# Recurrence and experts on one core: the turn of the keys moved ahead by most of a step, and the last token lists cut in two

## Chip, cores and metric

The kernel runs on one core of a Trainium2 chip, as one launch. The metric is the device time in microseconds (us). Engines are named as in the profile: PE (TensorE matmul) and PEld (its weight loads), DVE (VectorE), ACT (ScalarE), POOL (GpSimd) and SP (SyncE, whose queue issues most DMAs).

## What is computed

Two stages in sequence. A recurrence over 768 positions for 4 batches and 8 heads of width 48, and a mixture of 8 experts over the 3072 tokens that it gives, with at most one expert for each token:

```python
for t in range(S):                                   # attention, per batch and head
    cur = np.einsum('bhd,bhe->bhde', u[None] * kt, vt)
    y[:, :, t] = np.einsum('bhd,bhde->bhe', rt, state + cur)
    state = w[None, :, :, None] * state + np.einsum('bhd,bhe->bhde', kt, vt)
x = y.transpose(0, 2, 1, 3).reshape(B * S, H * D)
do_compute = x @ w_skip > 0                          # the other tokens pass unchanged
e_idx = np.argmax(x @ w_gate, axis=1)                # expert; its gate is the softmax value
y = gate_w[:, None] * (np.maximum(x @ w1[e], 0.0) @ w2[e])
out = x + y                                          # for the computed tokens
```

## The kernel before

**Steps.** The recurrence is cut into 12 chunks of 64 positions and two groups of heads, so 24 steps (`m` from 0 to 23). In a step PE makes `scores` (keys against queries, L503, into `ps_p`), `across` (queries against the carried state `sblk`, L563, into `ps_y`), `within` (masked scores `am` against the values `vkv`, L547, into `ps_y`) and `state` (keys against values, L527, into `ps_s`). POOL scales keys (`prep_t`: `kt`, L458) and queries (`prep_r`: `rd`, L443); ACT adds the scaled second half of `rd` (`prep_u`, L455), copies the finished rows (`take_x`: `xt`, L583) and the state (`sblk`, L540). PE turns the scaled keys into the bank `ps_t` (`turn_k`, L470) and DVE copies them to `kd` (`take_k`, L474), from which the scores two steps on are made; the first two keys are turned unscaled (`turn_raw`, L480) and scaled in the copy. DVE copies the scores under two masks (`mask_scores`, L514 and L515). Decay tables `w_d` are grown on DVE (L351) and turned by PE (`turn_table`, L362).

**Beside the steps.** The x of a finished chunk is written to the output by SP (L596), and also turned by PE (`turn_x`, L609, into `ps_t`) and copied by ACT (`xT`, L612). For every four tiles of 128 tokens come the logits (L623), copied, turned back and copied again (L631, L635, L636). A generator `route` (`tick` advances it: "v" pieces on DVE, "p" pieces on PE) then makes a token list of them: choice, ranks through matmuls into `pr`, one-hot rows `ol` and `vl`, and a matmul into `mine`, added to `lists`; `place` writes ids for the gathers (`gid`, `sid`) and the gates. `ROUTES` says at which step which tiles are listed. Expert 0's weights are loaded in 12 pieces during the steps and split into a high and a low part (ACT `whi`, POOL `wlo`, L123 and L124), expert 1's are loaded in steps 20 to 23.

**Bridge.** Behind step 23 the first 128 tokens of expert 0 are computed by the generator `first` (`single`: W1 at L210, turns L222, W2 L232, DVE's `hl` L225, `mix` L185), between the pieces of the last two lists; the second 128 tokens (`second`) need the last gather (L142). Expert 1 is split meanwhile (L134, L135, two pieces of three on DVE) and its tokens turned (`turn_one`, L162 to L164). The order of work is the order of the code: each engine takes its instructions in program order. The eight PSUM banks of the steps serve the experts too.

**Experts 1 to 7.** W1 at L171, rectifier at L175 and L176, W2 at L181, mix, and scatters (L188); the next expert is split beside it.

## Time and profile before

| | us |
|---|---|
| three runs | 310.77, 312.38, 317.28 (median 312.38) |
| the profiled execution | 311.63 |
| its span, first to last instruction | 309.8 |
| PE, DVE, ACT, POOL busy in the span | 273.6, 178.2, 138.4, 150.1 |

The profiled execution is 1.83 us longer than its span. Rows of the trace give the start in us from the span's start, the length, the engine, the line, the operation, output and inputs, and in brackets how long the engine idled before it and what ended that. PEclk is the clock that TensorE was granted, as a share of full speed.

### The profile page before, as it was taken

Reading aid. Unit: us, or ns where it says so; the run is one execution under the profiler, and the core shown is the slowest. Engines: PE = TensorE matmul, PEld = TensorE weight load, DVE = VectorE, ACT = ScalarE, POOL = GpSimd, SP = SyncE. Lnnn points to the kernel's source line nnn. Section 1 sums busy time; section 2 is a strip of 40 time slices with the busy share of each in tenths; the row PEclk is TensorE's granted clock in tenths of the full one; section 3 lists DMA queues with packets and bytes.
Section 4 is the critical chain, followed back from the end, with each engine's and each line's share of the span. In section 5 each row is a group of like instructions: output and inputs, shape, how many; then the busy total and the mean of one; then the engine's idle time right before and its main releaser. Section 6 shows DMA issues by size and latency. Waiting matters only on the chain.

```text
span 309.8 us, 9701 instructions
## 1 busy us (share of the span) xinstructions
PE 273.6 (88%) x4065; PEld 242.3 (78%) x4066; DVE 178.2 (58%) x377; ACT 138.4 (45%) x318; POOL 150.1 (48%) x159
## 2 busy tenths in 40 slices
PE   8699999899876997597976889999999999999991
PEld 3487767677765876475664779999999999999991
DVE  4536445445756376755573869486764938376310
ACT  4235545465533364323333738172654728173200
POOL 8366774748465264504136866435353444534111
PEclk9979999999997599959997999999999999999997
DMA  7368678788785263627993459571908355000000
GB/s 212 94 184 236 185 215 237 208 251 241 227 238 131 76 172 123 175 54 247 278 367 88 122 151 329 182 304 40 406 19 294 129 203 245 25 16 24 15 23 27
DMA packets 24582, 52.64 MB, mean 170 GB/s; under 512 B 3732, under 2 KB 11951, under 8 KB 24528
## 3 DMA queue, kind: packets, MB, share of 16 engines
...
q14 instruction: 19, 0.16, 0.2%
q10 hardware_dynamic: 272, 0.05, 0.1%
...
## 4 chain that ended last, share of the span: by engine, by line
PE 69%; DVE 15%; ACT 5%; issue 4%; DMA 4%; SPq 1%; POOL 0%; POOLq 0%; DVEq 0%
PE ps_p L503 10%; PE ps_s L171 10%; PE ps_y L181 9%; PE ps_p L181 9%; PE ps_p L171 5%; PE ps_y L171 5%; DVE kd L474 4%; PE ps_s L527 3%; PE ps_t L609 3%; PE ps_y L547 2%; PE ps_y L271 2%; DMA raw<-in_w_dram 2%; DMA xg<-out_dram,gid 2%; PE ps_t L470 2%; ACT rd L455 2%
## 5 line engine op out<-in xcount | busy, mean ns | idle before, releaser
L135 POOL TENSOR_TENSOR wlo<-raw,whi 128x512 fp32r<-128x512 f32 x28 | 37.8, 1348 | 39.2 <-ACT whi L134 20.2
L135 DVE TENSOR_TENSOR wlo<-raw,whi 128x512 fp32r<-128x512 f32 x56 | 50.5, 922 | 5.1 <-ACT whi L134 5.1
L134 ACT CAST whi<-raw 128x512 fp32r<-128x512 f32 x84 | 47.4, 624 | 0.0
L503 PE MATMUL ps_p<-rd,kd 48*64 48x128 f32 x768 | 30.6, 295 | 14.6 <-DVE kd L474 13.9
L514 DVE COPY_PREDICATED am<-below,ps_p 128x512 f32<-128x512 int8 x24 | 17.7, 738 | 36.7 <-PE ps_p L503 36.7
L503 PEld LDWEIGHTS ps_p<-rd,kd 48*64 48x64 f32 x768 | 24.0, 144 | 18.4 <-issue 11.7
L188 POOL DMA_INDIRECT out_dram<-xg,sid x16 | 17.4, 1087 | 35.5 <-DVE xg L185 30.1
L124 POOL TENSOR_TENSOR wlo<-raw,whi 128x512 fp32r<-128x512 f32 x12 | 15.6, 1299 | 38.2 <-ACT whi L123 35.4
L612 ACT COPY xT<-ps_t 128x384 f32<-128x384 f32 x23 | 11.0, 480 | 45.8 <-PE ps_t L609 45.8
L458 POOL TENSOR_TENSOR kt<-dm,w_t 128x384 f32<-128x384 f32 x24 | 24.4, 1019 | 13.5 <-ACT w_t L365 6.6
L142 POOL DMA_INDIRECT xg<-out_dram,gid x16 | 17.6, 1098 | 26.7 <-DVE em L788 12.2
L443 POOL TENSOR_TENSOR rd<-dm,w_d 112x512 f32<-112x512 f32 x22 | 29.0, 1318 | 0.0
L171 PE MATMUL ps_s<-xh,whi 128*128 128x256 f32 x84 | 23.8, 283 | 0.0
L171 PE MATMUL ps_s<-xl,whi 128*128 128x256 f32 x84 | 23.8, 283 | 0.0
L171 PE MATMUL ps_s<-xh,wlo 128*128 128x256 f32 x84 | 23.8, 283 | 0.0
L455 ACT ACTIVATE rd<-rd,uw 112x256 f32<-112x256 f32 x48 | 21.7, 505 | 2.3 <-POOL rd L443 2.3
L175 ACT ACTIVATE hh<-ps_p 128x512 fp32r<-128x512 f32 x7 | 4.2, 598 | 40.7 <-PE ps_p L171 40.7
L474 DVE COPY kd<-ps_t 112x512 f32<-112x512 f32 x22 | 15.1, 686 | 11.3 <-PE ps_t L470 5.6
L527 PE MATMUL ps_s<-vkv,kt 128*48 128x96 f32 x352 | 20.4, 262 | 0.0
L181 PE MATMUL ps_p<-whi,hh 128*128 128x384 f32 x56 | 19.3, 345 | 0.0
L181 PE MATMUL ps_y<-whi,hl 128*128 128x384 f32 x56 | 18.8, 336 | 0.0
L181 PE MATMUL ps_p<-wlo,hh 128*128 128x384 f32 x56 | 18.8, 336 | 0.0
...
## 6 DMA issues: line engine op xcount, KB each, us to landing
...
xg<-out_dram,gid POOLq DMA_INDIRECT x16, 3.5
out_dram<-xg,sid POOLq DMA_INDIRECT x16, 2.8
...
```

The source lines that it names most:

```text
L134: nc.scalar.copy(hi[:, s], t[:, s])
L135: (eng or nc.vector).tensor_tensor(lo[:, s], t[:, s], hi[:, s].bitcast(F32), ALU.subtract)
L142: ins = nc.gpsimd.indirect_dma_start(out=xg, out_offset=None, in_=out, in_offset=bass.IndirectOffsetOnAxis(ap=gid[:, q : q + 1], axis=0), ...
L171: nc.tensor.matmul(ph, a[:, c, fs], b[:, c, :], start=(k == 0), stop=(k == 3 * NCC - 1))
L181: nc.tensor.matmul(py, a, b[:, f, :], start=(k == 0), stop=(k == 3 * NFC - 1))
L443: eng.tensor_tensor(rd[:, :, :, 0], loaded[m][:DR, :RC].rearrange("p (n h c) -> p n h c", n=4, h=2), w_d[:, (m // NG) % NSUB, 0, half(m)][ ...
L455: nc.scalar.activation(rd[:, :, h, 1], rd[:, :, h, 0], AF.Copy, scale=uw[:, hp : hp + 1])
L458: nc.gpsimd.tensor_tensor(kts[m % 4][:, :, :, :D], loaded[m][:, RC:].rearrange("p (q k d) -> p q k d", q=NPAIR, d=D), w_t[:, (m // NG) % N ...
L474: nc.vector.tensor_copy(kds[m].rearrange("p k n c -> p (k n c)"), ps_t[:DR, :])
L503: nc.tensor.matmul(ps_p[lo(n), b, 2 * k * C : 2 * (k + 1) * C], kd[lo(a, D), k, n], rd[lo(a, D), NPAIR * b + q, h].rearrange("p s c -> p ( ...
L514: nc.vector.copy_predicated(shape(am[m % 2]), below, p[:, :, 0])
L527: nc.tensor.matmul(ps_s[g][lo(a, D), k * W2 : (k + 1) * W2], kt[:, q, 2 * h + a, :D], blocks[:, :, a, k], start=m < NG and k == 0, stop=Tr ...
```

## The change

The parts, in the order of the program:

- Warm-up matmuls on `ones`: 18 in a row become 9, and three before them two. In the opening the scores of step 0 come ahead of the table's turn; POOL builds the masks before it clears `kt`.
- The keys of the first four steps (`NRAW`), not two, are turned raw; their scaling copy is one instruction instead of two, with another order of heads in `kd`.
- A step is written in another order: across, turn of x, second half of `rd`, scores, masks, then at once turn and copy of k for step m+2, POOL's keys and queries, list matmuls, logits, within, `xt`, state, and the list work on DVE last.
- Lists are made of four tiles each, at steps 6, 10, 14, 18 and 22; before, the first was of eight, at step 11. `VTICKS` sets how many pieces a step takes.
- The last list (tiles 20 to 23) has a generator of its own: its logits are made with tokens on the partitions (`logits_here`), so they are not turned back, and its ids are placed and the two gathers issued before the gates are computed.
- The load of expert 2 waits for the second of these gathers.
- `first` runs to its end before `second` begins; behind it the PSUM pool is closed and eight new banks are declared for the experts.

```diff
-ROUTES = {11: (0, 8), 15: (8, 12), 19: (12, 16), 23: (16, 20)}
+ROUTES = {6: (0, 4), 10: (4, 8), 14: (8, 12), 18: (12, 16), 22: (16, 20)}
...
-NWARM = 18
+NWARM = 9
+NRAW = 4
+WARM1 = 4
+VTICKS = (2, 1, 3, 3)
...
         for j in range(pieces) if piece is None else (piece,):
-            (eng or nc.sync).dma_start(out=raw[e][:, j * q : (j + 1) * q], in_=w12[e, :, j * q : (j + 1) * q])
+            ins = (eng or nc.sync).dma_start(out=raw[e][:, j * q : (j + 1) * q], in_=w12[e, :, j * q : (j + 1) * q])
+            if after is not None:
+                tc.add_manual_dep(
...
-        for bank0 in (ps_t, ps_y[:, 0], ps_l):
+        for bank0 in (ps_t, ps_y[:, 0]):
             warm(1, bank0)
         warm(NWARM, ps_y[:, 1])
...
-        for t in kts:
-            nc.gpsimd.memset(t, 0.0)
-        clear_v(3, nc.gpsimd)
...
         below = lower("below", ALU.is_gt)
         eye = lower("eye", ALU.is_equal)
+        for t in kts:
+            nc.gpsimd.memset(t, 0.0)
+        clear_v(3, nc.gpsimd)
...
-            src = bank[:DR, :].rearrange("p (q h n c) -> p q h n c", q=2, h=2, n=2)
-            for h in range(2):
-                hp = (m % NG) * 2 + h
-                nc.vector.tensor_tensor(
...
+            nc.vector.tensor_tensor(
+                kds[m].rearrange("p (h q) n c -> p h (q n) c", h=2),
+                bank[:DR, :].rearrange("p (h q c) -> p h q c", h=2, c=C),
+                w_d[:, (m // NG) % NSUB, 1, half(m)].unsqueeze(2).to_broadcast([DR, 2, 4, C]),
+                ALU.mult,
+            )
...
-                        kd[lo(a, D), k, n],
+                        kd[lo(a, D), 2 * h + q if m < NRAW else k, n],
...
+        def logits_here(*ns):
+            for n in ns:
+                for c in range(NCC):
+                    nc.tensor.matmul(
+                        logit[:, (n % 4) * GW : (n % 4) * GW + E + 1],
+                        turned_x[n][:, c * P : (c + 1) * P],
...
-                if g1 == NT:
-                    place(1)
...
+        def last_route(g0, g1):
...
+            mx = small("mx")
+            nc.vector.tensor_reduce(mx, l8, AX.X, ALU.max)
+            nc.vector.tensor_tensor(eq[:, :, :E], l8, bc(mx), ALU.is_equal)
+            rdo = small("rdo", w=E)
...
+            yield
+            nc.tensor.matmul(pr[:, : n * E], tri, oh.rearrange(col), start=True, stop=False, skip_group_check=True)
...
+            vl = small("vl", F32R, NV3 * E)
+            ids = id1[:, g0:g1].unsqueeze(2).to_broadcast([P, n, E])
+            nc.vector.tensor_tensor(vl[:, :, :E], oh, ids, ALU.mult)
...
+            rk = small("rkp", w=E)
+            nc.vector.tensor_tensor(rk, pr[:, : n * E].rearrange("p (n e) -> p n e", e=E), oh, ALU.mult)
...
+            nc.vector.tensor_reduce(r1, rk, AX.X, ALU.add)
...
+            nc.vector.tensor_tensor(
+                ol, lane1[:, None, :].to_broadcast([P, n, P]), r1.unsqueeze(2).to_broadcast([P, n, P]), ALU.is_equal
+            )
...
+            for j in range(n):
+                nc.tensor.matmul(mine[:, :E], ol[:, j, :], vl[:, j, :E], start=(j == 0), stop=(j == n - 1))
...
+            last = lists[:, :, NJ - 1, :]
+            nc.vector.tensor_tensor(last[:, 0], mine[:, :E], last[:, 0], ALU.add)
+            place_ids(1)
+            yield
+            df = small("df", w=E)
+            nc.vector.tensor_tensor(df, l8, bc(mx), ALU.subtract)
+            nc.scalar.activation(df, df, AF.Exp)
+            nc.vector.tensor_scalar(over[:, g0:g1], r1, float(CAP), None, ALU.is_ge)
...
+            gw = small("gw")
+            nc.vector.tensor_reduce(gw, df, AX.X, ALU.add)
...
+            for v, val in ((1, gh), (2, gl)):
...
+            for j in range(n):
+                nc.tensor.matmul(
+                    mine[:, E : NV3 * E], ol[:, j, :], vl[:, j, E:], start=(j == 0), stop=(j == n - 1)
...
+            yield
+            nc.vector.tensor_tensor(
+                last[:, 1:], mine[:, E : NV3 * E].rearrange("p (v e) -> p v e", e=E), last[:, 1:], ALU.add
+            )
+            place_gates(1)
...
+        banks = {"py": [ps_p[:, 0]]}
...
         setup = setup_routes()
         turn_raw(0, ps_t)
         turn_raw(1, ps_y[:, 0])
-        turn_table(0, ps_l)
         prep_r(0, nc.vector)
         prep_u(0)
         take_raw(0, ps_t)
-        warm(4, ps_y[:, 1])
-        scores(0)
-        prep_t(0)
         prep_r(1, nc.vector)
         prep_u(1)
         take_raw(1, ps_y[:, 0])
+        scores(0)
+        turn_table(0, ps_l)
+        mask_scores(0)
+        grow(1)
+        warm(WARM1, ps_y[:, 1])
+        prep_t(0)
         prep_t(1)
         load_rk(3)
         load_v(2)
-        mask_scores(0)
-        grow(1)
-        turn_table(1, ps_l)
+        prep_r(2, nc.gpsimd)
         load_rk(4)
-        prep_t(2)
-        prep_r(2, nc.gpsimd)
         for m in range(NSTEP):
-            q = (m - 6) // 4
             if m + 3 < NSTEP:
                 load_v(m + 3)
             if m + 5 < NSTEP:
                 load_rk(m + 5)
+            across(m)
+            if m >= 2:
+                turn_x(m - 2)
+            if m + 2 < NSTEP:
+                prep_u(m + 2)
+            if m + 1 < NSTEP:
+                scores(m + 1)
+                mask_scores(m + 1)
+            if m + 2 < NRAW:
+                turn_raw(m + 2, ps_t)
+                take_raw(m + 2, ps_t)
+            elif m + 2 < NSTEP:
+                turn_k(m + 2)
+                take_k(m + 2)
+            if m < 3:
+                turn_table(1 + m, ps_l)
+                if m < 2:
+                    grow(2 + m)
+            if m == 0:
+                prep_t(2)
             if m + 3 < NSTEP:
                 prep_t(m + 3)
                 prep_r(m + 3, nc.gpsimd)
-            across(m)
-            if m + 1 < NSTEP:
-                scores(m + 1)
-                mask_scores(m + 1)
-            if m >= 2:
-                turn_x(m - 2)
+            tick("p")
+            if m >= 5 and m % 4 == 1:
+                logits((m - 5) // 4)
             if m >= 6 and m % 4 == 2:
-                logits(q)
-            if m >= 7 and m % 4 == 3:
-                logits_back(q)
-            tick("p")
-            if m + 2 < NSTEP:
-                prep_u(m + 2)
+                logits_back((m - 6) // 4)
             within(m)
             take_x(m)
             if m < NSTEP - NG:
                 state(m)
-            if m + 2 < NSTEP:
-                turn_k(m + 2)
-            if m in (0, 2):
-                grow(2 + m // 2)
-                turn_table(2 + m // 2, ps_l)
             if m in ROUTES:
                 begin_route(*ROUTES[m])
-            if m < 18:
-                tick("v", 2)
-            else:
-                tick("v", 3)
-                tick("p")
-                tick("v", 1)
-            if m + 2 < NSTEP:
-                take_k(m + 2)
+            tick("v", VTICKS[m % 4] + (m == NSTEP - 2))
...
+        last = last_route(NT - 4, NT)
+        next(last)
         run(1)
         turn_x(NT - 2)
         turn_x(NT - 1, ps_p[:, 1], nc.vector)
+        tick("p")
+        logits_here(20, 21)
+        tick("v", 4)
+        logits_here(22, 23)
+        take_logits(5, nc.vector)
+        assert not routes
+        next(last)
+        run(2)
+        next(last)
+        next(last)
         run(1)
-        tick("v", 4)
-        logits(5)
-        tick("p")
+        next(last)
+        next(last)
+        for q in (E, E + 1):
+            landed = gather(q, wpool)
         run(1)
-        tick("v", 4)
-        logits_back(5)
-        begin_route(NT - 4, NT)
+        next(last)
+        next(last)
         run(1)
-        tick("p")
...
+    def expert_banks():
+        pctx.close()
+        epsum = ctx.enter_context(tc.tile_pool(name="epsum", bufs=1, space=PSUM, reuse_waits="tile"))
+        for kind, k in (("ph", 4), ("pt", 2), ("py", 2)):
+            banks[kind] = [epsum.tile([P, 512], F32, name=f"{kind}{j}") for j in range(k)]
+            used[kind] = 0
 
...
-        load_expert(2, pieces=12)
+        load_expert(2, pieces=12, after=landed)
...
+            if g is second and n2 == 0:
+                for _ in first:
+                    pass
+                expert_banks()
...
-        for _ in first:
-            pass
```

How PE's order changes, in a plain step (before: step 4, after: step 8). In before, PE's queue has the turn of k (L470) behind state (L527):

```order
L563 MATMUL ps_y<-sblk_209,rd_370 64x48 x16
L503 MATMUL ps_p<-rd_438,kd_614 64x128 x16
L609 MATMUL ps_t<-ident,xt_498 128x128 x3
L547 MATMUL ps_y<-vkv_108,am_158 64x48 x16
L527 MATMUL ps_s_68<-vkv_108,kt_112 48x96 x8
L470 MATMUL ps_t<-ident,kt_114 112x128 x4
L563 MATMUL ps_y<-sblk_210,rd_438 64x48 x16
L503 MATMUL ps_p<-rd_538,kd_701 64x128 x16
```

In after, the same queue has it behind the scores (L477 behind L507; L567 is across, L612 the turn of x, L551 within, L531 state):

```order
L567 MATMUL ps_y<-sblk_199,rd_759 64x48 x16
L612 MATMUL ps_t<-ident,xt_880 128x128 x3
L507 MATMUL ps_p<-rd_860,kd_959 64x128 x16
L477 MATMUL ps_t<-ident,kt_114 112x128 x4
L551 MATMUL ps_y<-vkv_108,am_148 64x48 x16
L531 MATMUL ps_s_68<-vkv_108,kt_112 48x96 x8
L567 MATMUL ps_y<-sblk_200,rd_860 64x48 x16
L612 MATMUL ps_t<-ident,xt_880 128x128 x3
L507 MATMUL ps_p<-rd_962,kd_1071 64x128 x16
```

The turn of k moved from the end of the step to its middle, and the turn of x from behind the scores to ahead of them; both write `ps_t`.

DVE in a step with list work. In before, the copy `kd` (L474) is the last instruction of its step, behind the decay of the state (L537) and the list's comparisons:

```order
L514 COPY_PREDICATED am_159<-below,ps_p 128x512
L515 COPY_PREDICATED am_159<-eye,ps_p 128x512
L537 TENSOR_TENSOR ps_s_68<-ps_s_68,pw 112x384
L744 TENSOR_SCALAR hi_1648<-r_1545 128x8
L746 SCALAR_TENSOR_TENSOR lw_1650<-hi_1648,r_1545 128x8
L747 SCALAR_TENSOR_TENSOR hi_1648<-hi_1648,m_1437 128x8
L749 TENSOR_TENSOR ol_1647<-lane,lw_1650 128x1024
L474 COPY kd_1654<-ps_t 112x512
L514 COPY_PREDICATED am_158<-below,ps_p 128x512
L515 COPY_PREDICATED am_158<-eye,ps_p 128x512
```

In after, `kd` (L481) follows the two masks (L518, L519), and the list's operations (L764 to L774) stand behind it:

```order
L518 COPY_PREDICATED am_149<-below,ps_p 128x512
L519 COPY_PREDICATED am_149<-eye,ps_p 128x512
L481 COPY kd_1071<-ps_t 112x512
L764 TENSOR_TENSOR ol_1013<-lane,lw_1016 128x512
L769 TENSOR_TENSOR oj_1104<-blk,hi_1014 128x64
L774 TENSOR_TENSOR vl_1106<-oj_1104,id_195 128x4x16
L774 TENSOR_TENSOR vl_1106<-oj_1104,gh_1004 128x4x16
L774 TENSOR_TENSOR vl_1106<-oj_1104,gl_1005 128x4x16
L518 COPY_PREDICATED am_148<-below,ps_p 128x512
L519 COPY_PREDICATED am_148<-eye,ps_p 128x512
L481 COPY kd_1164<-ps_t 112x512
```

The copy passed the list work, which now stands ahead of the next masks instead.

DVE at the last list. In before, gates (`gl` L706, `gate_s` L790) and ids are made together:

```order
L708 TENSOR_TENSOR rkp_2674<-ps_l,oh_2647 128x32
L710 TENSOR_REDUCE r_2676<-rkp_2674 128x4
L723 TENSOR_TENSOR ol_2679<-lane_203,r_2676 128x512
L728 TENSOR_TENSOR vl_2681<-oh_2647,id_205 128x4x8
L728 TENSOR_TENSOR vl_2681<-oh_2647,gh_2670 128x4x8
L728 TENSOR_TENSOR vl_2681<-oh_2647,gl_2671 128x4x8
L738 TENSOR_TENSOR lists<-ps_l,lists 128x3x8
L786 TENSOR_SCALAR gid<-lists 128x8
L788 TENSOR_SCALAR em_2702<-lists 128x8
L789 SCALAR_TENSOR_TENSOR sid<-lists,em_2702 128x8
L790 TENSOR_TENSOR gate_s<-lists 128x8
L714 TENSOR_REDUCE sums_2678<-oh_2647 128x8
```

In after, the ids are summed (L863) and placed (L907 to L910) first, and the gates' operations (from L867) come behind:

```order
L851 TENSOR_TENSOR rkp_2687<-ps_l,oh_2672 128x32
L853 TENSOR_REDUCE r_2689<-rkp_2687 128x4
L855 TENSOR_TENSOR ol_2691<-lane_193,r_2689 128x512
L863 TENSOR_TENSOR lists<-ps_l,lists 128x8
L907 TENSOR_SCALAR gid<-lists 128x8
L909 TENSOR_SCALAR em_2704<-lists 128x8
L910 SCALAR_TENSOR_TENSOR sid<-lists,em_2704 128x8
L867 TENSOR_TENSOR df_2718<-lg,mx_2664 128x32
L869 TENSOR_SCALAR over<-r_2689 128x4
L872 TENSOR_REDUCE gw_2722<-df_2718 128x4
L873 TENSOR_SCALAR gw_2722<-gw_2722 128x4
L874 RECIPROCAL gw_2722<-gw_2722 128x4
```

What moved are the exponential, the gates' operations and two of the three products `vl`, from ahead of the ids to behind them.

## Rows read from the trace of the kernel before

**Rows 1.** The page's first line and its line on PE: busy us (share of the span), number of instructions.

```profile
span 309.8 us, 9701 instructions
PE 273.6 (88%) x4065; PEld 242.3 (78%) x4066; DVE 178.2 (58%) x377; ACT 138.4 (45%) x318; POOL 150.1 (48%) x159
```

**Rows 2.** The table of stages: stretch (us from the span's start), its length, then busy us (number of instructions) of PE, PEld, DVE, ACT and POOL, granted clock, mean busy share of the DMA engines, GB/s.

```profile
26.16:92.00 65.84, 59.58 (x1662) 47.90 (x1666) 35.71 (x66) 34.66 (x93) 41.18 (x44) 1.00 0.80 227
...
31.26:139.14 107.88, 92.82 (x2393) 75.38 (x2385) 62.09 (x138) 50.76 (x138) 57.87 (x54) 0.92 0.64 181
40.07:44.58 4.51, 4.18 (x119) 3.38 (x120) 2.18 (x3) 2.71 (x7) 3.48 (x4) 1.00 0.68 224
...
98.67:107.57 8.90, 8.90 (x131) 7.79 (x135) 3.06 (x10) 2.87 (x7) 0.83 (x1) 0.50 0.31 96
...
131.86:139.14 7.28, 7.07 (x120) 5.63 (x120) 4.20 (x14) 2.21 (x6) 0.00 (x0) 0.55 0.21 50
139.14:146.29 7.15, 5.58 (x164) 4.47 (x164) 3.29 (x16) 2.52 (x9) 2.34 (x3) 1.00 0.81 259
146.29:165.99 19.70, 13.90 (x106) 11.07 (x106) 11.08 (x52) 5.73 (x16) 6.35 (x6) 0.99 0.90 288
165.99:180.28 14.29, 11.93 (x57) 9.85 (x57) 11.12 (x13) 8.26 (x18) 11.76 (x10) 0.89 0.30 86
180.28:303.39 123.11, 123.07 (x877) 122.59 (x877) 73.80 (x115) 58.58 (x113) 51.30 (x41) 1.00 0.41 150
```

**Rows 3.** The chain that ended last, in two plain steps: start, us, what it was.

```profile
35.56 1.10 PE ps_p L503 x32
36.66 0.49 PE ps_t L609 x3
...
37.17 0.48 ACT xT L612
37.65 0.80 ACT rd L455 x2
38.46 0.37 ACT xt L583
...
39.23 0.70 DVE kd L474
...
40.07 1.10 PE ps_p L503 x32
```

**Rows 4.** Waits in the nineteen steps (31.26 to 139.14): who waited for whom, us in total, times, longest.

```profile
PE ps_p L503 <- DVE kd L474: 13.9, 18, 2.8
...
PEld ps_y L563 <- ACT xt L583: 1.2, 7, 0.2
```

**Rows 5.** The timeline of steps 17 to 22, PE's scores and DVE.

```profile
98.67 1.99 PE L503 MATMUL ps_p<-rd,kd 48*64 48x128 f32 x32 [2.83 <-DVE kd L474]
...
114.67 0.17 DVE L700 TENSOR_REDUCE gw<-df 128x4 f32<-128x32 f32 x1
...
116.68 1.00 DVE L747 SCALAR_TENSOR_TENSOR hi<-hi,m 128x4 f32<-128x4 f32 x1
...
118.21 0.68 DVE L474 COPY kd<-ps_t 112x512 f32<-112x512 f32 x1
...
119.03 1.10 PE L503 MATMUL ps_p<-rd,kd 48*64 48x128 f32 x32 [1.32 <-DVE kd L474]
...
120.19 0.73 DVE L514 COPY_PREDICATED am<-below,ps_p 128x512 f32<-128x512 int8 x1 [1.31 <-PE ps_p L503]
...
131.86 1.98 PE L503 MATMUL ps_p<-rd,kd 48*64 48x128 f32 x32 [1.60 <-DVE kd L474]
```

**Rows 6.** The timeline of the opening: PE and POOL.

```profile
2.77 5.32 PE L271 MATMUL ps_y<-ones 128*128 128x512 bf16 x18
...
8.02 1.08 PE L480 MATMUL ps_t<-ident,dm 128*48 128x128 f32 x16
...
15.36 1.60 PE L362 MATMUL ps_l<-ident,w_d 112*64 112x112 f32 x16 [2.35 <-DVE w_d L351]
...
17.55 1.00 POOL L458 TENSOR_TENSOR kt<-dm,w_t 128x384 f32<-128x384 f32 x1 [4.18 <-ACT w_t L365]
...
18.51 1.27 POOL L443 TENSOR_TENSOR rd<-dm,w_d 112x512 f32<-112x512 f32 x1
```

**Rows 7.** The last list in the timeline, from the last `xt` to the turned rows, and the page's line on the gathers (median us from issue to landing).

```profile
145.81 0.48 ACT L583 COPY xt<-ps_y 128x384 f32<-128x384 f32 x1 [0.18 <-PE ps_y L547]
...
158.70 0.17 DVE L786 TENSOR_SCALAR gid<-lists 128x8 uint32<-128x8 f32 x1
...
159.14 0.99 POOL L142 DMA_INDIRECT xg<-out_dram,gid  x1 [10.63 <-DMA raw<-in_w_dram]
...
164.87 0.55 PE L162 MATMUL ps_t<-ident,xg 128*128 128x128 f32 x3 [2.80 <-DMA xg<-out_dram,gid]
...
xg<-out_dram,gid POOLq DMA_INDIRECT x16, 3.5
```

**Rows 8.** The end of the bridge in the timeline: DVE and POOL.

```profile
176.73 2.40 DVE L135 TENSOR_TENSOR wlo<-raw,whi 128x512 fp32r<-128x512 f32 x1
177.28 1.30 POOL L135 TENSOR_TENSOR wlo<-raw,whi 128x512 fp32r<-128x512 f32 x1
...
180.06 0.60 DVE L185 SCALAR_TENSOR_TENSOR xg<-ps_y,gate_s,xg 128x384 f32<-128x384 f32 x1
```

More of the change, by code (lines that the diff above doesn't have):

```diff
@@ L73, in tile_wkv_moe @@
     wpool = ctx.enter_context(tc.tile_pool(name="wpool", bufs=1))
-    psum = ctx.enter_context(tc.tile_pool(name="psum", bufs=1, space=PSUM))
+    pctx = ExitStack()
+    psum = pctx.enter_context(tc.tile_pool(name="psum", bufs=1, space=PSUM))
     ps_p = psum.tile([P, 2, 512], F32, name="ps_p")
@@ L101, in tile_wkv_moe, with load_expert @@
     WCOLS = 2 * NCC * F
-    def load_expert(e, piece=None, pieces=4, eng=None):
+    def load_expert(e, piece=None, pieces=4, eng=None, after=None):
         if piece in (None, 0):
@@ L480, in turn_raw @@
                     nc.tensor.matmul(
-                        bank[lo(a, D), k * P : (k + 1) * P], src[:, k, a], ident, start=True, stop=True
+                        bank[lo(a, D), k * P : (k + 1) * P], src[:, k % 2, k // 2, a], ident, start=True, stop=True
                     )
@@ L542, in within @@
         def within(m):
-            t = vals_in[m]
+            t = vals_in.pop(m)
             for k in range(4):
@@ L615, in turn_x @@
             turned_x[n] = xT
-        LG = 64
-        back = ps_l[:, 384:]
+        logit, back = ps_l[:, 64:192], ps_l[:, 384:]
         def logits(q):
@@ L630, in logits @@
             lt = wk.tile([P, P], F32, tag="lt", name=f"lt{q}")
-            nc.scalar.copy(lt, ps_l[:, LG : LG + P])
+            nc.scalar.copy(lt, logit)
             turned_x["lt"] = lt
@@ L638, in logits_back, with take_logits @@
             )
-            seen[0] = 4 * q + 3
+        def logits_here(*ns):
[4 more added lines that the diff above has]
+                        turned_x[n][:, c * P : (c + 1) * P],
+                        wg_sb[:, c, : E + 1],
+                        start=c == 0,
+                        stop=c == NCC - 1,
+                    )
+        def take_logits(q, eng):
+            eng.tensor_copy(
+                lg[:, 4 * q : 4 * q + 4, :], logit.rearrange("p (j e) -> p j e", j=4)[:, :, : E + 1]
+            )
         NV3 = 3
@@ L784, in place, with place_gates, place_ids @@
+        def place(j):
+            place_ids(j)
+            place_gates(j)
+        def place_gates(j):
+            c = slice(j * E, (j + 1) * E)
+            nc.vector.tensor_tensor(gate_s[:, c], lists[:, 1, j], lists[:, 2, j], ALU.add)
+        def place_ids(j):
             c = slice(j * E, (j + 1) * E)
@@ L805, in tick @@
                     routes[0][1] = nxt
-        banks = {
-            "ph": [ps_s[0], ps_s[1], ps_p[:, 1], ps_y[:, 1]],
-            "pt": [ps_t, ps_l],
-            "py": [ps_p[:, 0], ps_y[:, 0]],
-        }
+        banks = {"py": [ps_p[:, 0]]}
         used = dict.fromkeys(banks, 0)
@@ L927, in tile_wkv_moe @@
         turn_x(NT - 1, ps_p[:, 1], nc.vector)
+        tick("p")
[8 more added lines that the diff above has]
+        next(last)
         run(1)
-        tick("v", 4)
-        logits(5)
-        tick("p")
+        next(last)
+        next(last)
+        for q in (E, E + 1):
+            landed = gather(q, wpool)
         run(1)
-        tick("v", 4)
-        logits_back(5)
-        begin_route(NT - 4, NT)
+        next(last)
+        next(last)
         run(1)
-        tick("p")
-        tick("v", 4)
-        run(2)
-        tick("p")
-        tick("v", 4)
-        run(2)
-        tick("p")
-        tick("v", 4)
-        run(1)
-        tick("p")
-        tick("v", 4)
-        assert not routes
-        gather(E, wpool)
-        gather(E + 1, wpool)
-        order = [q for e in range(2, E) for q in ((E + e,) if e < NEARLY else (e, E + e))]
+        next(last)
+        next(last, None)
+        order = [q for e in range(2, E) for q in ((E + e,) if e < NEARLY else (e, E + e))]
+    def expert_banks():
[4 more added lines that the diff above has]
+            used[kind] = 0
     with ExitStack() as mctx:
```

74 lines of the change are left out of this document (64 added, 10 removed).

## The prediction

> **What bounds the kernel now.** I read the page's first lines, then a table of stages, then the chain of waits inside two plain steps, then the waits that end late and the instructions around them. The span is 309.8 us, PE (TensorE) busy for 88% [rows 1]. The table cuts the span by what runs [rows 2]: an opening of 31.26 us, nineteen steps of the recurrence (from the scores of step 4 to those of step 23) of 107.88, a last step of 7.15, a bridge of 19.70 and 14.29 in which expert 0 is computed and the last rows are gathered, and the experts from 180.28 on. There PE is busy 123.07 of 123.11 us, and the change moves nothing in that stage or behind it. A gain has to come from before 180.28.
>
> In the nineteen steps PE is busy 92.82 of 107.88 us [rows 2]. Of the 15.06 that are idle one wait has 13.9: scores waiting for `kd`, the copy of the turned keys [rows 4]. The chain of a plain step shows why [rows 3]: scores, the turn of x, its copy `xT` on ACT (ScalarE), the scalings of `rd`, the copy `xt`, and only then, behind another ACT copy, DVE's (VectorE's) copy `kd` of 0.70 and the scores again, 4.51 us a round. PE is busy for 4.18 of such a round (from 40.07 on, [rows 2]). With list work on DVE it is worse: `kd` starts at 118.21, behind list work, and the scores at 119.03 waited 1.32 us [rows 5]. In two steps PE runs at the lower of its two clocks, 1.2 GHz (granted 0.50 and 0.55): 8.90 and 7.07 us busy [rows 2].
>
> **The change part by part.** *Steps.* The turn of k for step m+2 and its copy come directly behind scores and masks of step m+1, so `kd` is ready most of a step before it is read, and the wait of 13.9 us goes. What is late next is `ps_t`: the bank now passes from x to the keys and back within a step, and the next step's turn of x waits until `kd` is copied out. Behind that turn stand the scores, and DVE waits for those. DVE needs, from the start of the scores, 1.16 us to the first mask, 1.50 for two masks, 0.70 for the copy: 3.36 [rows 5, 3]. PE comes to that turn of x after a round of 4.18 less the turn itself, 0.49: 3.69. Some 0.3 us are left, and list work must fit into what DVE has free, 4.18 minus 1.50 minus 0.70, about 2 us. The largest piece of a four-tile list, ten small operations, took from 114.67 to 116.68, 2.0 us, and one of them then 1.00 where its like took 0.17 [rows 5]. The second new wait: across now follows state directly, and needs `xt`, 0.48 long; the turn of k no longer covers it. That wait cost 1.2 us in seven cases before [rows 4]; state (0.8 in such a round) is still there, so I put it at nothing, and at 0.2 a step if ACT is late. ACT's scalings of `rd` move ahead of the masks' step, behind POOL's (GpSimd's) `rd`, which was made a step earlier: nothing.
>
> The sum for the steps: PE's busy 92.82, less what the low clock added. The step at 98.67 would hold, at full clock, 4.18 and 0.77 of list matmuls, so 8.90 is 3.95 too much; the one at 131.86 has 7.07 for 4.18, 2.89 too much. Both began behind waits of 2.83 and 1.60 us for `kd` [rows 5], which go. That leaves 86.0, a gain of 21.9. I give back 1.2 (the idle time that was not `kd`'s) and 1.0 for each of four lists that overrun DVE's 2 us. Steps: minus 16.7. Bounds: minus 21.9 with no overrun; minus 7.6 if the turn of x inherits the plain step's 0.33 in all nineteen (6.3) and each list costs 2.0 (8.0).
>
> *Opening.* Ten warm-up matmuls go, of the kind of which eighteen took 5.32 us and held back the first turn until 8.02 [rows 6]; I count 2.0. Scores of step 1 no longer stand behind the table's turn, which waited 2.35 for DVE at 15.36, and two more keys are turned raw, without waiting for POOL's `kt` (1.00) [rows 6]; but POOL's `rd` (1.27) still stands in that chain: 1.5. Minus 3.5; bounds minus 6.0 (all of both) and minus 1.0 (POOL's chain alone decides).
>
> *Last step.* Logits and list matmuls leave it, rank matmuls come in; PE has 1.57 idle of 7.15 [rows 2]. Minus 0.8, between 0 and minus 1.2.
>
> *Bridge, first part.* From the start of step 23's `xt` (145.81) the last `gid` took 13.1 us (158.70 and 0.17), its rows were turned at 164.87 [rows 7]. One of the two lists in that chain now ends some 1 us behind `xt`, the logits come out unturned, and the ids are placed before any gate is computed. At the lengths that these operations have in the trace (0.17 to 0.69) I count 7.2 us from `xt` to `gid`; issue 1.0 and landing 3.5, the median [rows 7] (the last one took 5.7 beside expert 2's load, which now waits for it): rows there at 12. But PE has the rest of expert 0's first tile ahead of them: it was busy 13.90 in this stretch [rows 2], and with a wait for each of two `hl` I make it 15, and 1.1 for turn, cast and handover. So 16.1 for 19.70: minus 3.6. Bounds: minus 6.7 if the gather alone decides, 0 if the waits for `hl` eat it. The new banks cost nothing: the second tile's W1 needs the one that the first mix reads (0.60 [rows 8]), and turn and cast cover that.
>
> *Bridge, second part*, 14.29 at a mean clock of 0.89 [rows 2]: 3.1 us at half, worth 1.6. The low clock came behind 2.80 idle [rows 7], and PE now arrives from work: minus 1.3. Its end is DVE's, split pieces and mixes, the last at 180.06 [rows 8]; bounds 0 and minus 3.5.
>
> The load of expert 2 moves on SP's queue to behind the gathers, 13 us after `xt`; only expert 3 stands behind it. 3.1 MB at the 288 GB/s of the bridge [rows 2] are 10.9 us, and the first piece is wanted some 31 us after `xt`. Nothing; were those 7 us used up, each one late would be one lost.
>
> Total: 3.5 + 16.7 + 0.8 + 3.6 + 1.3 = 25.9 off the profiled execution's 311.63 (1.83 more than its span): 285.7, say 286. The median of the runs shown, 312.38, lies 0.75 above that execution.
>
> On DVE's pieces: one beside POOL's of 1.30 took 2.40 us [rows 8]. The Trainium skill, GPSIMD Engine Reference, section 1, says that POOL shares its SBUF interfaces with VectorE and contends with VectorE instructions that have two SBUF inputs, as `wlo` has; the trace agrees. By that rule the pieces that stretch stay as long, and the second part of the bridge keeps its end at DVE.
>
> **The rivals.** *Memory sets the pace.* From 26.16 to 92.00 the queues moved 227 GB/s at share 0.80 [rows 2], with 13 steps begun to begun in 65.4 us 1.14 MB a step. At 4.55 us a step that is 250 GB/s at a share of 0.88. For: loads of a step would queue more. Against: the bridge moved 288. If it holds fifteen steps 0.35 longer, 5.3 us: 291.
>
> *DVE becomes the bound.* The steps gain 7.6 only: 295. For: stretched operations [rows 5, 8]. Against: DVE is busy 62.09 of 107.88 us [rows 2].
>
> *The wait only changes its name.* One bank serves keys and x. If the turn of x inherits all 13.9 us and the low clock, opening, last step and bridge gain 9.2: 302; without the bridge's 4.9, 307, no change. Against: 0.3 us of slack by the durations above.
>
> *The low clock, slower than before.* If the new short waits (`ps_t`, `xt`) bring PE to 1.2 GHz, each such step costs 2.89 us (the step at 131.86). From nine of nineteen steps the gain is gone; twelve give 286 + 34.7 = 321. For: two steps fell behind waits. Against: the plain round had 0.33 idle and was granted 1.00, as was all of 26.16 to 92.00 [rows 2]. The Trainium skill, TensorE: Matmul & The Clock Gate, section "A second HAM failure mode: psum-queue depth-cycling", tells of a kernel whose frequent short idles between groups of matmuls made the clock swing. By that rule this rival would be likelier; the trace does not bear it out at 0.33.
>
> **How the numbers follow.** Forecast 286, its own range 279 to 293: 0.55. Memory, 291: 0.16. DVE, 295: 0.17. The wait renamed: 0.07, of which 0.04 ends within 2%. Low clock: 0.05. Two per cent, 6.2 us, is about what a measurement of this kernel can tell from no change. Faster by more: 0.91; within: 0.04; slower: 0.05. The range goes from 278 (steps and bridge half way to their better bounds) to 299 (DVE's case with the opening at its worse bound and some of the bridge lost).
>
> **What would show it.** Right: no scores that wait for `kd`; rounds of 4.2 to 4.9 us; scores of step 23 near 119; the last gather issued some 8 us behind `xt`; the experts' first matmul near 154. Wrong: turns of x that wait for `kd` by more than 0.5 in many steps; across behind `xt`; steps granted 0.5; an expert stage longer than 123.1 because expert 2 came late.

## The result, and the profile after

The changed kernel takes 299.82 us (median of four runs, 299.49 to 301.5) against 313.11 for the kernel before beside it; the ratio is 0.961 (95% interval 0.954 to 0.968). It is faster, but by about half of what was forecast, and lies just above the range. The profiled execution is 299.87 us with a span of 298.2, so 11.6 us of span are gone where 25.9 were worked out. The times of the runs further down are medians of all executions of a kernel; some executions lie 1.5% or more above the kernel's fastest, and the ratios leave these out. The page's first lines:

```profile
span 298.2 us, 9706 instructions
PE 272.5 (91%) x4084; PEld 242.8 (81%) x4084; DVE 199.2 (67%) x402; ACT 141.8 (48%) x317; POOL 150.7 (51%) x159
```

PE is as busy as before [rows 1], but DVE has 21 us more of busy time for 25 more instructions. The table of stages, cut at the same events as [rows 2] (scores of step 4, scores of step 23, end of the last `xt`, first W1 of the second tile, first matmul of the experts, last matmul):

```profile
0.00:27.29 27.29, 24.68 (x490) 17.84 (x490) 18.02 (x40) 12.96 (x28) 20.85 (x46) 1.00 0.66 197
27.29:133.27 105.98, 92.97 (x2423) 75.86 (x2422) 78.61 (x177) 54.55 (x139) 59.12 (x55) 0.92 0.64 184
133.27:138.67 5.40, 4.57 (x143) 3.65 (x142) 3.85 (x19) 2.49 (x8) 3.00 (x3) 1.00 0.88 226
138.67:157.31 18.64, 17.06 (x100) 14.08 (x99) 10.40 (x43) 5.10 (x14) 3.99 (x4) 0.91 0.66 213
157.31:168.09 10.78, 10.24 (x57) 8.87 (x57) 8.96 (x11) 8.17 (x18) 8.66 (x8) 1.00 0.91 329
168.09:291.09 123.00, 123.00 (x878) 122.52 (x877) 78.70 (x114) 58.56 (x113) 54.08 (x44) 1.00 0.42 153
```

| stage | before | after | forecast | measured |
|---|---|---|---|---|
| opening | 31.26 | 27.29 | -3.5 | -3.97 |
| nineteen steps | 107.88 | 105.98 | -16.7 | -1.90 |
| last step | 7.15 | 5.40 | -0.8 | -1.75 |
| bridge, first part | 19.70 | 18.64 | -3.6 | -1.06 |
| bridge, second part | 14.29 | 10.78 | -1.3 | -3.51 |
| experts and what follows | 129.52 | 130.11 | 0 | +0.6 |

Almost all of the shortfall is in the steps. PE's waits there, whole stretch, in us, times, longest:

```profile
PE ps_t L612 <- DVE kd L481: 8.4, 5, 2.9
PE ps_l L779 <- DVE vl L774: 2.5, 2, 2.0
PE ps_t L477 <- ACT xT L615: 1.4, 4, 0.5
PE ps_l L697 <- DVE oh L695: 0.7, 2, 0.4
```

The wait of the scores for `kd` [rows 4] is gone as forecast, and PE still waits 13.0 us: the turn of x now waits for `kd` instead, four times by 1.2 to 2.9 us. A plain round takes 4.22 us, and three rounds run for a part at the lower clock (granted 0.50, which is 1.2 GHz), each behind one of these waits (of 2.12, 2.86 and, for the list matmuls, 1.97 us):

```profile
112.74:116.96 4.22, 4.22 (x121) 3.47 (x120) 2.98 (x6) 2.43 (x6) 3.66 (x4) 1.00 0.81 232
...
56.90:65.68 8.78, 8.28 (x149) 6.63 (x148) 4.91 (x12) 2.67 (x7) 3.38 (x4) 0.61 0.51 141
81.16:87.97 6.81, 6.81 (x148) 5.62 (x148) 3.29 (x12) 3.00 (x7) 0.00 (x0) 0.75 0.26 82
102.32:112.74 10.42, 8.46 (x148) 6.78 (x147) 6.07 (x12) 3.18 (x8) 4.19 (x4) 0.67 0.45 132
```

Nine of the nineteen rounds take 4.91 us or less. The other ten, all with list work, take 66.7 together. The timeline of one of them shows what DVE does there (`L759` to `L762` are products and comparisons of 128x4 numbers):

```profile
50.91 1.28 POOL L132 TENSOR_TENSOR wlo<-raw,whi 128x512 fp32r<-128x512 f32 x1 [4.40 <-ACT whi L131]
51.05 1.16 DVE L759 TENSOR_SCALAR hi<-r 128x4 f32<-128x4 f32 x1
52.14 1.00 POOL L465 TENSOR_TENSOR kt<-dm,w_t 128x384 f32<-128x384 f32 x1
52.25 0.91 DVE L761 SCALAR_TENSOR_TENSOR lw<-hi,r 128x4 f32<-128x4 f32 x1
53.10 1.29 POOL L450 TENSOR_TENSOR rd<-dm,w_d 112x512 f32<-112x512 f32 x1
53.20 1.20 DVE L762 SCALAR_TENSOR_TENSOR hi<-hi,m 128x4 f32<-128x4 f32 x1
54.33 0.71 DVE L518 COPY_PREDICATED am<-below,ps_p 128x512 f32<-128x512 int8 x1
...
54.81 1.26 POOL L132 TENSOR_TENSOR wlo<-raw,whi 128x512 fp32r<-128x512 f32 x1 [0.43 <-ACT whi L131]
55.07 0.73 DVE L519 COPY_PREDICATED am<-eye,ps_p 128x512 f32<-128x512 int8 x1
...
55.70 0.67 DVE L481 COPY kd<-ps_t 112x512 f32<-112x512 f32 x1
...
56.04 1.93 POOL L465 TENSOR_TENSOR kt<-dm,w_t 128x384 f32<-128x384 f32 x1
56.29 0.68 DVE L764 TENSOR_TENSOR ol<-lane,lw 128x512 fp32r<-128x512 f32 x1
...
56.42 0.55 PE L612 MATMUL ps_t<-ident,xt 128*128 128x128 f32 x3 [2.12 <-DVE kd L481]
```

Three tiny operations, each begun beside a POOL operation, end with it: 52.21 and 52.19, 53.16 and 53.14, 54.40 and 54.39. The second mask, which reads PSUM, keeps its 0.73 us beside POOL's 1.26. So `kd` comes 2 us late, and PE waits 2.12. It goes the other way too: POOL's `kt`, 1.00 us long at 52.14, takes 1.93 at 56.04, beside DVE's `ol`, which keeps its 0.68. For `L762` the view of that one line gives shortest, median and longest in ns:

```profile
L762 DVE SCALAR_TENSOR_TENSOR hi<-hi,m x4: 161/1198/2141, 53.2 to 124.3; 128x4 f32<-128x4 f32 x4
```

Summed over all 112 list operations in the nineteen steps, each less the shortest of its own line, tiles and shape, that is 18.6 us of 40.7 (twenty are over twice their shortest); by the same sum before it was 3.2 of 22.3 (four of 77). Each of the twenty ends 0.02 to 0.08 us behind the end of a POOL operation, and so do the four.

### The profile page after: what moved, and what is told of

Same layout as the page of the kernel before. It is cut to its first block, busy times and chain, and to the rows that moved or that the text cites. A ratio compares the mean times of both kernels' runs of the same rounds, so it can differ in the third digit from the quotient of the medians.

```text
span 298.2 us, 9706 instructions
## 1 busy us (share of the span) xinstructions
PE 272.5 (91%) x4084; PEld 242.8 (81%) x4084; DVE 199.2 (67%) x402; ACT 141.8 (48%) x317; POOL 150.7 (51%) x159
## 4 chain that ended last, share of the span: by engine, by line
PE 65%; DVE 19%; issue 5%; DMA 3%; POOL 2%; ACT 2%; SPq 1%; POOLq 0%; DVEq 0%
PE ph L179 20%; PE py L189 20%; PE ps_p L507 4%; PE ps_s L531 3%; DVE am L518 3%; DVE kd L481 3%; PE ps_y L551 2%; PE ps_t L612 2%; PE ps_y L567 2%; PE ps_l L625 2%; DVE vl L774 2%; DMA raw<-in_w_dram 2%; PE ps_t L477 2%; DVE hi L762 2%; PE pt L170 2%
## 5 line engine op out<-in xcount | busy, mean ns | idle before, releaser
L179 PE MATMUL ph<-xh,whi 128*128 128x256 f32 x168 | 47.7, 284 | 0.0
L179 PE MATMUL ph<-xh,wlo 128*128 128x256 f32 x168 | 47.6, 283 | 0.0
L179 PE MATMUL ph<-xl,whi 128*128 128x256 f32 x168 | 47.6, 283 | 0.0
L183 ACT ACTIVATE hh<-ph 128x512 fp32r<-128x512 f32 x28 | 16.7, 598 | 53.1 <-PE ph L179 53.1
L189 PE MATMUL py<-whi,hh 128*128 128x384 f32 x112 | 38.2, 341 | 0.0
L189 PE MATMUL py<-whi,hl 128*128 128x384 f32 x112 | 37.7, 337 | 0.0
L189 PE MATMUL py<-wlo,hh 128*128 128x384 f32 x112 | 37.7, 336 | 0.0
L518 DVE COPY_PREDICATED am<-below,ps_p 128x512 f32<-128x512 int8 x24 | 17.5, 731 | 27.1 <-PE ps_p L507 27.1
L184 DVE SCALAR_TENSOR_TENSOR hl<-ph,hh 128x512 fp32r<-128x512 f32 x28 | 19.3, 688 | 21.4 <-ACT hh L183 21.4
L179 PEld LDWEIGHTS ph<-xh,whi 128*128 128x128 f32 x168 | 32.3, 192 | 0.0
L179 PEld LDWEIGHTS ph<-xl,whi 128*128 128x128 f32 x168 | 32.3, 192 | 0.0
L179 PEld LDWEIGHTS ph<-xh,wlo 128*128 128x128 f32 x168 | 32.2, 192 | 0.0
L150 POOL DMA_INDIRECT xg<-out_dram,gid x16 | 16.8, 1052 | 19.8 <-DVE em L909 16.0
L507 PE MATMUL ps_p<-rd,kd 48*64 48x128 f32 x768 | 26.7, 277 | 0.0
```

The source lines that it names most:

```text
L150: ins = nc.gpsimd.indirect_dma_start(out=xg, out_offset=None, in_=out, in_offset=bass.IndirectOffsetOnAxis(ap=gid[:, q : q + 1], axis=0), ...
L179: nc.tensor.matmul(ph, a[:, c, fs], b[:, c, :], start=(k == 0), stop=(k == 3 * NCC - 1))
L184: nc.vector.scalar_tensor_tensor(hl, ph, 0.0, hh.bitcast(F32), ALU.max, ALU.subtract)
L189: nc.tensor.matmul(py, a, b[:, f, :], start=(k == 0), stop=(k == 3 * NFC - 1))
L507: nc.tensor.matmul(ps_p[lo(n), b, 2 * k * C : 2 * (k + 1) * C], kd[lo(a, D), 2 * h + q if m < NRAW else k, n], rd[lo(a, D), NPAIR * b + q, ...
L518: nc.vector.copy_predicated(shape(am[m % 2]), below, p[:, :, 0])
```

## Experiments

Theory A: a list operation on DVE that reads SBUF stands still while a POOL operation runs; `kd` is late by that, and PE's waits and its low clock follow. Rivals: the lists are too much work at any speed (B), memory sets the pace (C), the new order itself (D), the shared bank (E).

**e1, the stall by itself.** Behind the last expert, for five kinds of operation, with `f(8)` alone and `f(k)` beside POOL:

```diff
+        for f, k in ((two, 24), (one_, 24), (red, 24), (frm, 8), (mixed, 8)):
+            f(8)
+            meet()
+            beside(4)     # four 128x512 subtractions on GpSimd
+            f(k)
+            meet()
```

> The changed kernel with a stretch added behind the last expert: VectorE repeats one small operation, first 8 alone and then 24 (or 8 long ones) while GpSimd makes four 128x512 subtractions from SBUF; five kinds in turn: product of two SBUF tiles (128x32), comparison of one SBUF tile with a constant (128x4), reduction (128x32), copy from PSUM (128x512), product of a PSUM and an SBUF tile (128x512). Theory A (VectorE's operations from SBUF stand still while a GpSimd operation runs): beside GpSimd the first two kinds have single instructions of 0.8 to 1.3 us that end with the GpSimd operation, against 0.16 to 0.20 alone; the two kinds with PSUM keep their length within 5%; the reduction, never long in the trace, keeps 0.17 to 0.2. Rival B (the list pieces are simply too much work for VectorE): no kind longer than 1.3 times its length alone.

```profile
296.23 1.78 DVE L1201 TENSOR_TENSOR sml<-sml 128x32 f32<-128x32 f32 x8
298.05 8.35 DVE L1201 TENSOR_TENSOR sml<-sml 128x32 f32<-128x32 f32 x24
298.16 1.03 POOL L1192 TENSOR_TENSOR bn<-bn 128x512 f32<-128x512 f32 x1 [3.00 <-DVE bn L1197]
298.27 0.97 DVE L1201 TENSOR_TENSOR sml<-sml 128x32 f32<-128x32 f32 x1
306.42 1.60 DVE L1205 TENSOR_SCALAR sml<-sml 128x4 f32<-128x4 f32 x8
308.06 7.88 DVE L1205 TENSOR_SCALAR sml<-sml 128x4 f32<-128x4 f32 x24
308.23 1.04 POOL L1192 TENSOR_TENSOR bn<-bn 128x512 f32<-128x512 f32 x1 [5.51 <-DVE sml L1205]
308.27 1.02 DVE L1205 TENSOR_SCALAR sml<-sml 128x4 f32<-128x4 f32 x1
315.98 1.73 DVE L1209 TENSOR_REDUCE sml<-sml 128x4 f32<-128x32 f32 x8
317.75 5.26 DVE L1209 TENSOR_REDUCE sml<-sml 128x4 f32<-128x32 f32 x24
334.58 5.77 DVE L1217 TENSOR_TENSOR bn<-pt,bn 128x512 f32<-128x512 f32 x8
340.38 5.77 DVE L1217 TENSOR_TENSOR bn<-pt,bn 128x512 f32<-128x512 f32 x8
```

Three times the length alone would be 5.34 and 4.80; the products of two SBUF tiles took 8.35 and the comparisons 7.88, 3.0 and 3.1 us more beside 4.5 us of POOL. Reductions (5.26 for 5.19), copies from PSUM (5.77 for 5.76) and products with a PSUM operand lost nothing. The timeline groups equal operations, and a window of 0.5 us shows a single one (the rows with x1): 0.97 us where one alone takes 0.19, and 1.02 for 0.17, ending at 299.24 and 309.29, where POOL's operations end at 299.19 and 309.27. Four of each kind are stretched in this way, one for each POOL operation, as A expected; the ones between keep their length.

**e2, no lists in the steps** (`route` returns before its operations).

> The changed kernel with the lists of tiles 0 to 19 left out (their VectorE and TensorE operations; the lists stay empty, the gathers fetch row 0). Theory A and rival B alike (it is the list work on VectorE, stretched or not, that holds the steps): scores of step 4 to scores of step 23 take 81 to 84 us against 106.0, no turn of x waits over 0.4 us for kd, granted clock 1.00, kernel 275 to 279. Rival C (memory sets the pace at about 4.55 us a step): 86 to 88 us for the nineteen steps, kernel 280 to 283. Rival D (the new order itself holds PE, lists or not): over 95 us.

287.33 us (one run):

```profile
26.57:114.46 87.89, 85.94 (x2386) 69.21 (x2385) 42.78 (x65) 53.86 (x135) 55.79 (x54) 0.98 0.77 222
```

No turn of x waited over 0.2 us for `kd`, and 18.1 of the 105.98 us were gone; D falls. The size was missed: 87.9, not 81 to 84. PE alone is busy for 85.94 us of it, partly at low clock behind a 1.2 us pause in the middle of its scores that no wait in the trace explains. So the result lies in the band of C, but PE's own work fills that band, and this run cannot tell the two apart; e5 does.

**e3, POOL held to the time of the masks.**

```diff
-                prep_t(m + 3)
+                prep_t(m + 3, sc[-1] if m >= 6 else None)   # waits for the scores
```

> The changed kernel with one wait added: from step 6 on GpSimd's scaled keys (and so the scaled queries behind them) start only when PE has made the scores of the step, so that these 2.3 us lie beside VectorE's masks and copy, which read PSUM. The amount of work is the same on both engines. Theory A: the time by which list operations exceed their shortest length falls from 18 us in the nineteen steps to 4 to 8 (the low parts of expert 0 on GpSimd remain), the waits of the turn of x for kd from 8.4 to under 4, kernel 288 to 294. Rival B (amount of work): nothing moves by more than 2 us, 298 to 302.

291.16 us (290.17 to 292.4). The same work on both engines, only later on POOL, and 8.7 us less: B falls. PE's waits for `kd`:

```profile
PE ps_t L619 <- DVE kd L485: 3.4, 4, 1.9
```

The stall, by the sum above, fell only to 13.3 us, not to 4 to 8: 5.6 us of it are in operations that end with the low parts of expert 0, which remain, and nearly all of the rest in some that end with POOL's held operations, which late pieces of a list still meet.

**e4, x turned into spare columns of the y banks,** so that `ps_t` holds keys alone (`turn_x` ahead of `across`, two copies).

> The changed kernel with x turned into the unused columns of the y banks, ahead of across, and copied by ScalarE in two instructions; ps_t then holds keys alone. Theory A (VectorE is late, whatever waits for it): the waits of the turn of x (8.4 us) come back as waits of the scores for kd or of the turn of k, less 0.5 for each of five, kernel 295 to 299. Rival E (the shared bank ps_t is the cause): 8.4 us of waits and the low clock behind them go, kernel 284 to 290.

308.16 us (305.01 to 311.04), slower than the changed kernel and outside both expectations. From the scores of step 5 to those of step 23:

```profile
PE ps_y L567 <- ACT xT L616: 19.8, 18, 1.8
```

Across now waits for the copy of other columns of its bank: the edit made another wait, and it does not decide about E. e5 does.

**e5, the small tiles of the lists in PSUM.** POOL, the order, the list operations and their sizes stay (one copy of `rev` into PSUM is added ahead of the steps); of two SBUF operands one now lies in unused columns of `ps_l`:

```diff
-            mx = small("mx")
+            mx = inps(288)             # columns 288 to 291 of ps_l
...
-            lw = small("lw")
+            lw = inps(336)
...
-            oj = small("oj", w=NSL)
+            oj = inps(192, NSL)        # and rdo, m2, gw, r1, sums, hi, rev
```

> The changed kernel, GpSimd as it is (nothing held), but the small tiles of the list work (maxima, ranks, block numbers, one-hot blocks) lie in unused columns of the PSUM bank ps_l, so that hardly any VectorE operation of a list reads two SBUF tiles. Same operations, same order, same sizes. Theory A: list operations keep 0.15 to 0.7 us beside GpSimd, the excess falls from 18 us to under 4, the waits of the turn of x for kd from 8.4 to under 2; scores of step 4 to those of step 23 take 88 to 93 us, kernel 283 to 289. Rival B (amount of work): 298 to 302. Rival F (PE, ACT and VectorE now wait for each other on the bank ps_l): excess gone, but new waits on ps_l of over 5 us, 291 to 300.

284.95 us (283.42 to 287.91), ratio to before 0.906 (0.897 to 0.916):

```profile
27.36:117.24 89.88, 86.36 (x2423) 71.02 (x2422) 61.85 (x178) 54.37 (x139) 57.03 (x55) 1.00 0.75 218
```

```profile
PE ps_t L613 <- DVE kd L482: 0.2, 1, 0.2
```

```profile
L768 DVE SCALAR_TENSOR_TENSOR ps_l<-hi,ps_l x4: 166/166/166, 50.6 to 107.5; 128x4 f32<-128x4 f32 x4
```

`L768` is what `L762` was: 166 ns every time. The stall is 0.2 us in all, PE's wait for `kd` 0.2, the clock 1.00 throughout, and the nineteen steps take 89.88 us with the same 2423 matmuls. `ps_t` is still shared, so E falls; the lists are the same work, so B does; PE has no wait for `ps_l` there, so F does. PE is busy for 86.36 of the 89.88 us, and none of its waits ends with a load, so that memory (C) can hold it by 3.5 us at most. **e6** (e5 with POOL held as in e3):

> The tiles of the lists in PSUM as in e5, and GpSimd's scaled keys held until the scores as in e3. Theory A: both take away the same loss, so the second adds little to the first: within 2 us of e5, 282 to 289. If the two together gain clearly more than e5 (over 3 us), something besides the blocked operations of the lists is made late by GpSimd.

284.06 us (283.15 to 285.8), within 2 us of e5, as A has it: holding POOL has nothing left to add.

**e7, the kernel before, with the lists' tiles in PSUM** (the same edit in the old order).

> The kernel before, in its own order, with the small tiles of the list work in unused columns of ps_l (of the eight-tile list all but the one-hot blocks). In its trace list operations exceed their shortest length by about 4 us in the steps. Theory A (the new order put the list work where GpSimd runs, and so met the stall; in the old order little of it was paid): a gain of 0 to 4 us, 308 to 313. Rival I (the stall cost both kernels alike, and the new order itself brings little): a gain of 10 us or more, below 302.

309.24 us, ratio to before 0.983 (0.974 to 0.992): 4.8 us by the medians, 2.6 to 8.1 by the interval, a little over A's 0 to 4 and short of I's 10. The stall in its trace, by the sum above, fell from 3.2 us to 0.1. So the stall costs some 5 us in the old order and 15 in the new (299.82 to 284.95), and without it the change brings some 24 us (309.24 to 284.95).

**e8 to e12, the bridge of e5.** There PE is granted 0.53 from 126 to 133 us, behind 24 logits matmuls of 9 columns and waits for DVE's list work. e8 makes the last logits in the old form:

```diff
-        logits_here(20, 21)
         tick("v", 4)
-        logits_here(22, 23)
-        take_logits(5, nc.vector)
+        logits(5)
+        logits_back(5)
```

> The kernel of e5 with the last list's logits made as the others are: gate weights standing, 24 matmuls of 128 columns, then a copy, a turn back and a copy; not 24 matmuls of 9 columns with x standing. In e5 PE is granted 0.50 from 126.7 to 133.8, behind those narrow matmuls. Theory G (the narrow matmuls bring the low clock): granted clock 0.95 or more from the last xt to the second tile's first W1, 2 to 4 us less there, kernel 281 to 283. Rival H (the waits around the last list bring it, whatever the logits' form): a stretch of 0.50 remains, and the two copies and the turn back cost 0.5 to 1.5 us: 285 to 287.

282.46 us (281.71 to 285.33): 2.5 us less by the medians, as under G, but with a stretch at 0.50 left, as under H, so that neither holds as it stands. The ratios to the kernel before, 0.902 (0.897 to 0.907) and e5's 0.906 (0.897 to 0.916), overlap. e11 adds ten matmuls on `ones` in the waits:

> The kernel of e8 with ten matmuls on ones (512 columns) put where PE waits for VectorE around the last list: three ahead of the 16th to 20th tiles' list matmuls, five ahead of the last logits, two ahead of their turn back. e8 was granted 0.50 for 3.4 us from 125.3 on, behind 2 us in which PE was busy 0.6. Theory H (the waits bring the low clock): granted 1.00 there, 1 to 2 us less, 280.5 to 281.5. Theory G (the kind of matmul does): the stretch stays, 282 to 283.5.

282.71 us (280.87 to 286.35). The clock where e8's falls, and then e11's first part of the bridge, whole:

```profile
122.00:124.00 2.00, 0.61 (x4) 0.52 (x4) 1.89 (x11) 0.12 (x1) 0.00 (x0) 1.00 1.05 335
124.00:126.00 2.00, 1.60 (x27) 1.23 (x28) 0.00 (x0) 0.46 (x2) 0.00 (x0) 0.70 1.00 363
126.00:128.00 2.00, 2.00 (x6) 1.29 (x4) 1.25 (x7) 0.00 (x0) 0.00 (x0) 0.50 1.05 392
```

```profile
122.97:142.03 19.06, 15.92 (x110) 11.92 (x110) 10.67 (x43) 5.58 (x16) 3.99 (x4) 1.00 0.56 185
```

Filled, the waits leave the clock at 1.00, and the time does not move: e8's first part took 18.63 us with 3.4 at the lower clock, e11's 19.06 with none; one filler waited 1.4 us for DVE's copy out of the bank that it writes. e11's profiled execution also has a stretch at 0.50 in the steps, from 51.75 to 55.16, behind a 1.15 us pause of PE in the middle of its turn of x that no wait explains. e9 puts a part of W1 between the two halves of the narrow logits:

> The kernel of e5 with the first third of the first tile's W1 half between the two halves of the narrow logits matmuls, where PE waited 0.9 us for VectorE; the number of matmuls is the same. Theory G: the narrow matmuls stay, so a low clock remains, but in part: 0 to 2 us less, 283 to 285. Rival H (the wait brings it): the wait is covered and the clock stays at 1.00, 3 us less, 281 to 282.

289.08 us (285.33 to 292.4), no faster than e5 (283.42 to 287.91) and against both. PE was at 0.50 from 119.5 to 136.6, from before the place of the edit; why is open. e10 lets expert 2's load go at once:

> The kernel of e5 with expert 2's load no longer waiting for the last gather. The prediction put the load's delay at nothing and took from it a shorter landing of the last gathers (3.5 for 5.7 us). If that holds: second tile's first W1 up to 2 us later where PE waits for the gather, expert stage unchanged, kernel 285 to 287. Rival J (PE is not waiting for the gather there): within 0.7 us of e5.

284.39 us (283.62 to 290.1): J, the load's wait costs nothing and brings nothing that these runs can tell. Last, e12:

> The kernel of e11 with GpSimd's scaled keys held until the scores, as in e3 and e6: the combination that the runs so far point to. e6 lay 0.9 below e5. 280 to 281.5 if that adds up, within 1 us of e11 if it does not.

282.93 us (281.21 to 283.89): it does not add up, though its profiled execution, 283.46 us, was granted 1.00 through steps and bridge. e8, e11 and e12 cannot be told apart; all are 17 us below the changed kernel and some 10% below the one before (e8: 0.902, 0.897 to 0.907).

## Why the prediction was wrong

**The step that failed** is one term of the sum for the steps: "1.0 for each of four lists that overrun DVE's 2 us". From the base of 86.0 that I had worked out for PE, the steps came to 105.98, so 20 us were to be given back where I had 5.2 (1.2 for waits that stay, 4.0 for the lists): 13.0 of waiting and 6.6 of low clock (92.97 us of PE, against 86.36 for the same matmuls in e5). With the stall taken away (e5) the steps are 16.1 us shorter: 4.0 for each of the four lists where I had 1.0. The base was right to 0.4, and e5's 89.88 is below the 91.2 of my sum: the mechanism of the reorder is as forecast, and the size of DVE's overrun is where it went. That e5's 284.95 is so near to my 286 is partly luck: its first part of the bridge took 1.4 us more than before (21.10 for 19.70), where I had 3.6 less, and the other stages made up for it.

```profile
122.88:143.98 21.10, 18.38 (x100) 15.46 (x100) 10.94 (x45) 5.10 (x13) 3.99 (x4) 0.84 0.55 183
```

**How it was mis-sized.** I took the lengths of list operations from one piece in the old order, 2.0 us, one of them 1.00 where its like took 0.17 [rows 5], and did not ask what had stretched that one. It was the stall, which e1 shows by itself and e3 and e5 take away: it ran from 116.68 to 117.68, beside this row of the kernel before.

```profile
116.67 1.00 POOL L458 TENSOR_TENSOR kt<-dm,w_t 128x384 f32<-128x384 f32 x1 [1.39 <-issue]
```

I named the sharing of SBUF interfaces for the low parts in the bridge, where it cost PE 0.5 us at most (one wait for DVE's `xl`, behind a `wlo` of 2.48 us), and not for the lists, where it cost 15 us. The Trainium skill has the rule more sharply than in the section that I named: SBUF — State Buffer, section "SBUF: two separate sides", says that whichever of the two engines starts first holds the shared ports for its whole instruction and the other is blocked, where VectorE's instruction has two SBUF inputs or runs in a two-port mode. On the blocking the rows above agree (54.40 and 54.39); on who comes first they do not always, since `kt` begins at 56.04 and `ol` at 56.29, and it is `kt` that is stretched. Whether the blocked comparison of one SBUF tile in e1 (7.88 us for 4.80) runs in a two-port mode no run here shows.

**What was right in the steps.** No scores wait for `kd`; a plain round is 4.22; what came late next is `ps_t`, by the turn of x, as named. With 0.3 us of slack the stall went on to PE: 11.6 of its 13.0 us of waits are for DVE's `kd`, `vl` and `oh`. Of the rivals, DVE as the bound came nearest (295, at 0.17); its mark against, DVE's busy time in the kernel before, counted for nothing, since the new order stretched that time (62.09 to 78.61 us). The low clock came too, three stretches, each behind a wait that the stall made, and in e5 it is gone from the steps; e2 and e11 have one stretch each in the steps behind an unexplained pause of 1.2 us. Memory does not set the pace.

**Opening:** 3.97 for 3.5. **Last step:** 1.75, beyond my bound of 1.2; PE is busy for 4.57 us of it where it was for 5.58, and idle for 0.83 where it was for 1.57.

**Bridge, first part:** 1.06 for 3.6. From the start of `xt` the last `gid` took 10.1 us, where I had 7.2:

```profile
138.19 0.48 ACT L587 COPY xt<-ps_y 128x384 f32<-128x384 f32 x1 [0.53 <-PE ps_y L551]
...
139.99 1.49 PE L645 MATMUL ps_l<-wg_sb,xT 128*128 128x9 f32 x12
...
141.84 1.48 PE L645 MATMUL ps_l<-wg_sb,xT 128*128 128x9 f32 x12 [0.37 <-DVE sums L731]
148.10 0.17 DVE L907 TENSOR_SCALAR gid<-lists 128x8 uint32<-128x8 f32 x1
```

I had taken the unturned logits as a saving. Their 24 narrow matmuls take 2.97 us, where 24 of the old form took 0.86 in a step of e2 at full clock, and the clock is 0.91 in this part. So PE was busy 17.06 us where I had 13.90. That is not all of it: with the old form of the logits the part still takes 18.63 us (e8: PE busy for 15.17, the rest waits, most of them for DVE's work on the last list and none for `hl`), and with the clock at 1.00 as well 19.06 (e11). My 15 for PE counted waits for `hl` alone; what would give the 2.5 us back stays open. **Second part:** 3.51 for 1.3, at the better bound: the clock stayed at 1.00, and the end was not DVE's, as I had put it. Before, the experts' first matmul waited for DVE's mix out of its bank:

```profile
180.28 0.36 PE L171 MATMUL ps_p<-xh,whi 128*128 128x256 f32 x1 [1.35 <-DVE xg L185]
```

After, it follows PE's own W2 with no wait (168.09), into one of the eight new banks, which I had put at nothing; no run has them alone. e10 bears out that expert 2's load costs nothing.
